# Turning the fetched rows of a routed FFN: TensorE transposes replaced by a trip through memory and a block transpose

## The chip, the cores and the metric

The kernel runs on one core of a Trainium2 chip. The metric is the device time of one execution in microseconds (us); the time of a kernel is the median of its runs. A core has five engines that run beside each other, each through its own list of instructions in order: TensorE (PE in the profile; its weight loads are listed as PEld), VectorE (DVE), ScalarE (ACT), GpSimd (POOL) and SyncE (SP), which issues most of the transfers. Transfers run on 16 DMA engines; SP, ACT and POOL each have a queue of their own into them.

## The reference

The first part is attention with pooled queries: 8 batches, 8 heads, 1152 keys, head size 64, all in f32. Neighbouring queries are averaged in pairs, so 576 queries are left.

```python
q_pool = q.reshape(B, H, S // 2, 2, D).mean(axis=3)
attn = softmax(scale * q_pool @ k.T)          # per batch and head
x = (attn @ v), heads side by side            # (8, 576, 512)
```

The second part is a routed feed-forward network (FFN). In each batch the 128 of the 576 rows with the highest score are updated, and the others are kept as they are.

```python
scores = x @ w_gate
top_idx = np.argpartition(-scores[b], 128)[:128]
xe = x[b, top_idx]                            # 128 rows of 512
h = np.maximum(xe @ w1, 0.0)                  # w1: 512 x 1024
ye = h @ w2                                   # w2: 1024 x 512
out[b, top_idx] = xe + sigmoid(scores[b, top_idx])[:, None] * ye
```

## The kernel before

**Attention.** The work goes by pairs of heads, 4 pairs a batch and 32 in all, and each pair by two halves of 288 queries; so there are 64 halves, `h` in `run`. In a half PE computes the scores of all keys (`scores`, L883, 72 recorded matmuls of 64x64 tiles) and ACT turns them into exponents (L890). PE then multiplies the exponents of the half before by the values (`weighted`, L901), and ACT copies the result out of PSUM (L909). POOL and DVE sum the exponents (L922, L927, L937); DVE turns results with block transposes of 32x32 (L980, and L770 and L774 for the next pair's keys and queries). PSUM is handed out by `banks()` in turn from four tiles.

**The order of the work** is written out by hand. One half emits, in this order: scores, the groups or sums of an earlier pair on ACT (L952 or L967), a place called "mid", the folding of the exponents, a place called "sums", the next pair's keys and queries, weighted, and a place called "end". Each batch has one generator, `routed`, which does its routing and FFN piece by piece. `units` lets it run at a place until it yields the next mark: "mid" and "sums" name the place at which it goes on, and `True` stands for "end". So where the generator yields decides in which half, and behind which instructions, a piece lies on each engine.

**Routing.** For a batch the generator ranks the rows by counting larger scores on DVE (L1159 to L1178), sends the ranks through memory so that every partition holds all of them (L1208 and L1212, on SP), and searches the row of each rank (L1243). It then fetches the 128 chosen rows from the output in memory with an indirect transfer on POOL, the gather (L1270), into `xe`, one row a partition. The rows were put there by `stored` (L1038, SP). In the last batch the ranks go through PE instead (L1220, L1229).

**Before the FFN the rows must be turned**, since a matmul sums over partitions: `xeT` holds the 512 features in four chunks `c` of 128 partitions, and the 128 rows beside each other. Four transposes on PE (L1288) do it, and ACT copies them from PSUM (L1291). In batches 0 to 5 this stands at "mid", two halves after the gather. Feature `c * 128 + p` lies on partition `p` of chunk `c`, and the weights w1 are loaded to match (L691).

**FFN.** Batches 0 to 5 are taken two at a time: `layers_of_two` makes sums of quarters on POOL (L1400), seven products in place of eight on PE (L1434), copies on ACT (L1442), and sums on DVE (L1447). Batches 6 and 7 run alone through `layers` (L1309, L1329). Updated rows go back by an indirect transfer on POOL (L1376).

**The tail.** After the last half `run` lists the rest by hand: `older` is the unit of batches 4 and 5, `old` that of batch 6, `new` that of batch 7, and `pieces(unit, n)` lets a unit run for n yields. There DVE copies batch 7's scores (L1140), counts its ranks (from L1168) and compares (L1220); PE turns these into indices (L1229), and batch 7's gather follows. Batch 6's transposes lie on PE between batch 5's second layer (L1434) and batch 6's first (L1309).

Of the kernel before, what the change touches and what calls it, by code (L numbers as in the profile page):

```python
# [10 lines left out]
P = 128  # L11
BLK = 32

G = 3
F32 = mybir.dt.float32
# [12 lines left out]
def _any_scores(  # L28
# [451 lines left out]
    in_pair = [(j, t) for j in range(2) for t in range(NF)] + [(0, NF)]  # L480
    upcoming = load_pair(*pairs[0])
    run(prepare_pair(upcoming))
    preparing = iter(())
    routing = iter(())
# [23 lines left out]
    for n, (b, hp) in enumerate(pairs):  # L508
        pair = upcoming
        run(preparing)  # L510
        if hp == 0:
            x = xpool.tile([P, NT, Dm], F32, name="x")
        for i, (j, t) in enumerate(in_pair):
            now = {"pair": pair, "j": j, "t": t, "x": x}
            advance(now)
            if two is not None and two["t"] == NF and two["pair"]["hp"] == NPAIR - 1:
                run(routing)
                routing = routed(two["pair"]["b"], two["x"])
            one, two = now, one
            if i == 0 and n + 1 < len(pairs):  # L520
                upcoming = load_pair(*pairs[n + 1])
                preparing = prepare_pair(upcoming)
            if n == 0 and i == 0:
                load_weights()
            if i >= 3:
                next(preparing, None)
            next(routing, None)
    for _ in range(2):
        advance(None)
        one, two = None, one  # L530
    run(routing)
    run(routed(B - 1, x))


class _Plain:
# [152 lines left out]

    def weight_loads(self):

        w1 = self.w1_in.rearrange("(c p) f -> p c f", p=P)  # L691
        w2 = self.w2_in.rearrange("(c p) d -> p c d", p=P)
        for c in range(0, self.NFC, 2):
            yield self.nc.sync.dma_start(self.w2[:, c : c + 2, :], w2[:, c : c + 2, :])
        for c in range(self.ND):
            yield self.nc.sync.dma_start(self.w1[:, c, :], w1[:, c, :])
# [375 lines left out]
    def routed(self, b, part):  # L1072


        nc, ffn, Sp, NT, NF = self.nc, self.ffn, self.Sp, self.NT, self.NF
        tiles = [(t, P if t < NF else self.TAIL) for t in range(NT)]
        mid = "mid" if b < self.B - 2 else True
# [136 lines left out]
        for s0, w in self.slots:  # L1214
            index = ffn.tile([P, 1], I32, name="index", bufs=4)
            own_gate = ffn.tile([P, 1], F32, name="own_gate", bufs=4)
            if b == self.B - 1:

                pick = ffn.tile([P, NT, P], F32, name="pick", bufs=1)
                nc.vector.tensor_tensor(  # L1220
                    out=pick[:, :, 0:w],
                    in0=self.token_line[:, s0 : s0 + w, 0].unsqueeze(1).broadcast_to([P, NT, w]),
                    in1=rank[:, :].unsqueeze(2).broadcast_to([P, NT, w]),
                    op=ALU.is_equal,
                )
                yield True
                ps = self.banks()[:, 0, 0:2]
                for t, rows in tiles:
                    nc.tensor.matmul(  # L1229
                        ps[0:w, :],  # L1230
                        lhsT=pick[0:rows, t, 0:w],
                        rhs=meta[0:rows, t, :],
                        start=(t == 0),
                        stop=(t == NT - 1),
                    )
                nc.scalar.copy(index[0:w, :], ps[0:w, 0:1])
                nc.scalar.copy(own_gate[0:w, :], ps[0:w, 1:2])
            else:
                yield True

                def search(of, to):
                    at = ffn.tile([P, NT, P], F32, name="pick", bufs=1)
                    nc.vector.scalar_tensor_tensor(  # L1243
                        out=at.rearrange("p t i -> p (t i)").rearrange("p (i t) -> p i t", t=NT)[0:w],
                        in0=lines[0:w, :, 0, :],
                        scalar=self.token[0:w, s0 // P : s0 // P + 1],
                        in1=of[0:w, :, :],
                        op0=ALU.is_equal,
                        op1=ALU.mult,
                        accum_out=to[0:w, :],  # L1250
                    )

                found = self.small.tile([P, 1], F32, name="found_token")
                search(self.token_line, found)
                nc.vector.tensor_scalar(
                    out=index[0:w, :],
                    in0=found[0:w, :],
                    scalar1=float(b * Sp),
                    scalar2=None,
                    op0=ALU.add,  # L1260
                )
                if b == self.B - 2:
                    search(lines[:, :, 1, :], own_gate)

                yield "sums" if b < self.B - 2 else True
            if b == self.B - 1:
                xe = ffn.tile([P, self.Dm], F32, name="lines", bufs=1)
            else:
                xe = ffn.tile([P, self.Dm], F32, name="xe", bufs=3)
            nc.gpsimd.indirect_dma_start(  # L1270
                out=xe[0:w, :],
                out_offset=None,
                in_=rows_out,
                in_offset=bass.IndirectOffsetOnAxis(ap=index[0:w, 0:1], axis=0),
                bounds_check=(b + 1) * Sp - 1,
                oob_is_err=False,
            )
            yield True
            if b < self.B - 2:
                search(lines[:, :, 1, :], own_gate)  # L1280
                yield True
            if b != self.B - 2:
                yield mid

            xeT = ffn.tile([P, self.ND, P], F32, name="xeT")
            pv = self.banks()[:, 0, :].rearrange("p (c n) -> p c n", n=P)
            for c in range(self.ND):
                nc.tensor.transpose(  # L1288
                    pv[:, c, 0:w], xe[0:w, c * P : (c + 1) * P], self.ident[0:w, 0:w]
                )  # L1290
            nc.scalar.copy(xeT[:, :, 0:w], pv[:, 0 : self.ND, 0:w])  # L1291
            token = {"xe": xe, "xeT": xeT, "gate": own_gate, "index": index, "rows": rows_out, "w": w, "b": b}
            if b >= self.paired:
                yield mid
                yield from self.layers(token)
            elif b % 2 == 0:
                self.first_of_two = token
            else:
                yield from self.layers_of_two([self.first_of_two, token])
# [259 lines left out]
    def run(self):  # L1559
        nc = self.nc  # L1560
# [11 lines left out]
        sums = self.weight_sums() if self.paired else iter(())  # L1572
        for h in range(n_halves):
            n, s = divmod(h, 2)
# [22 lines left out]
            if h > 1:  # L1597

                of = halves[h - 2 - s]["pair"]
# [33 lines left out]
        def pieces(unit, n=None):  # L1633
            for i, _ in enumerate(unit):
                if i + 1 == n:
                    break
# [3 lines left out]
        old = left.pop() if left else iter(())  # L1640
        older = left.pop() if left else iter(())
        assert not left
        self.gated(halves[-3])
        self.weighted(halves[-1])
        self.drained(halves[-1])
        self.multiplied(halves[-2])
# [7 lines left out]
        _, new, _ = self.routing.pop()  # L1654

        pieces(new, 1)
        for half in (halves[-3], halves[-1]):
            self.divided(half["pair"])
            self.stored(half["pair"])
        pieces(older, 2)  # L1660
        pieces(new, 1)
        pieces(older, 1)
        pieces(new, 3)
        pieces(old, 1)
        pieces(older, 4)
        pieces(old, self.NFC // 2)
        pieces(new, 1)
# [73 lines left out]
```

## Time and profile before

| | us |
|---|---|
| median of three runs | 689.79 (689.55 to 689.9) |
| the profiled execution | 694.23 |
| its span, from first to last instruction | 692.4 |
| PE busy in the span | 683.8 (99%), 10000 matmuls |
| DVE busy | 530.3 (77%) |
| ACT busy | 461.5 (67%) |
| POOL busy | 514.8 (74%) |
| L1288, the transposes before the FFN, batches 0 to 6 | 4.6 busy, 28 matmuls |
| L1291, their copies, all batches | 4.6 busy, 8 copies of 0.573 |
| mean clock granted to PE | 0.996 of full speed |

The page gives busy time by engine and by line. A chain of work that ended last is followed back from the last instruction, at each step to what released it. Lists in order of time give, for one stretch, the start, the duration, engine, line and operation, the tile written and the tile read, their shapes (partitions x elements), how many instructions were merged, and in brackets how long the engine had been idle before and what ended that. An engine with idle time isn't a bound; a bound engine's chain has none.

### The profile page before, as it was taken

The numbers are of one execution on the slowest core, as the hardware profiler recorded it, in microseconds if no ns is written. First come the engines' busy times: TensorE is split into PE (matmuls) and PEld (weight loads), VectorE is DVE, ScalarE is ACT, GpSimd is POOL, SyncE is SP. The second block draws the span as 40 slices with busy tenths as digits, with TensorE's granted clock in tenths as the row PEclk, the third lists the DMA queues.
The fourth block names the chain that finished last, engine by engine and source line by source line (L and its number), as shares of the span: only waits on it lengthen the run. The fifth ranks groups of instructions, "written<-read, shape, count | busy, mean of one in ns | idle before, by whom it ended". The sixth has DMA issues, their size and how long they took to land.

```text
span 692.4 us, 23690 instructions
## 1 busy us (share of the span) xinstructions
PE 683.8 (99%) x10000; PEld 531.5 (77%) x10000; DVE 530.3 (77%) x837; ACT 461.5 (67%) x1005; POOL 514.8 (74%) x503
## 2 busy tenths in 40 slices
PE   8999999999999999999999999999999999999996
PEld 5667899989777978786768877777667885877876
DVE  3867888997999696686598986595868997589830
ACT  4677778777877773857777777583877777576220
POOL 4778888887897793866998888383989888559241
PEclk9999999999999999999999999999999999999999
DMA  8888888687868887743968787763597878344211
GB/s 166 154 172 168 175 185 181 145 152 151 162 137 164 165 151 132 205 90 71 214 122 182 123 174 128 132 175 69 119 199 174 141 154 157 80 115 118 51 47 36
DMA packets 392197, 97.56 MB, mean 141 GB/s; under 512 B 376977, under 2 KB 377105, under 8 KB 390801
## 3 DMA queue, kind: packets, MB, share of 16 engines
q1 hardware_dynamic: 390624, 91.46, 65.4%
q0 software_dynamic: 1296, 4.20, 1.9%
q8 instruction: 80, 1.31, 0.8%
q10 hardware_dynamic: 160, 0.30, 0.2%
q14 instruction: 37, 0.29, 0.2%
HBM read 80.13 MB, written 15.78 MB: 139 GB/s over the span
## 4 chain that ended last, share of the span: by engine, by line
PE 95%; DMA 2%; issue 1%; POOL 1%; ACT 0%; POOLq 0%; SPq 0%; DVE 0%
PE ps L901 41%; PE ps L883 41%; PE ps L1434 11%; PE ps L1309 1%; DMA out_dram<-xe,index 1%; DMA p<-in_k_dram 1%; PE ps L1288 1%; DMA out_dram<-lines,index_part 0%; POOL out_dram L1376 0%; PE ps L850 0%; PE ps L833 0%; ACT p L890 0%; PE ps L1229 0%; POOL xe L1494 0%; PE ps L1131 0%
## 5 line engine op out<-in xcount | busy, mean ns | idle before, releaser
L890 ACT ACTIVATE p<-ps 128x576 f32<-128x576 f32 x576 | 320.4, 693 | 4.9 <-PE ps L883 4.9
L922 POOL TENSOR_TENSOR acc<-p 128x576 f32<-128x576 f32 x192 | 274.2, 1456 | 31.8 <-ACT p L890 31.3
L883 PE MATMUL ps<-qT,kT 64*64 64x288 f32 x4608 | 296.9, 405 | 0.7 <-DVE token L637 0.5
L901 PE MATMUL ps<-p,v_sb 64*64 64x288 f32 x4608 | 295.4, 403 | 0.0
L883 PEld LDWEIGHTS ps<-qT,kT 64*64 64x64 f32 x4608 | 211.9, 133 | 70.0 <-ACT p L890 10.4
L901 PEld LDWEIGHTS ps<-p,v_sb 64*64 64x64 f32 x4608 | 215.2, 133 | 65.1 <-ACT p L890 11.4
L927 DVE TRANSPOSE_TENSOR_REDUCE fold<-p 128x54 f32<-128x1728 f32 x64 | 126.0, 1969 | 41.6 <-ACT p L890 40.9
L927 DVE TRANSPOSE_TENSOR_REDUCE fold<-acc 128x54 f32<-128x1728 f32 x64 | 124.7, 1949 | 22.9 <-POOL acc L922 22.8
L909 ACT COPY two<-ps 128x576 f32<-128x576 f32 x64 | 40.8, 638 | 135.7 <-PE ps L901 121.7
L911 POOL TENSOR_TENSOR av<-two 128x288 f32<-128x288 f32 x64 | 51.2, 800 | 81.1 <-ACT two L909 78.5
L990 POOL TENSOR_TENSOR prod<-avb,w_gate 128x288 f32<-128x288 f32 x64 | 51.3, 802 | 0.2
L980 DVE STREAM_TRANSPOSE avb<-av 128x288 f32<-128x288 f32 x64 | 29.0, 454 | 26.8 <-POOL av L911 23.9
L767 POOL TENSOR_TENSOR qp<-qb 128x576 f32<-128x576 f32 x31 | 43.7, 1409 | 7.8 <-DMA qb<-in_q_dram 7.8
L770 DVE STREAM_TRANSPOSE kT<-kb 128x1152 f32<-128x1152 f32 x31 | 42.0, 1356 | 0.0
L967 ACT ACTIVATE sums<-total,tiny 32x18 f32<-32x18 f32 x124 | 38.2, 308 | 4.6 <-DVE total L958 2.8
L1027 POOL TENSOR_TENSOR x<-avb,rec 128x576 f32<-128x576 f32 x30 | 34.8, 1159 | 0.0
L1178 DVE SCALAR_TENSOR_TENSOR pick<-sc_row,gate_sc,before 128x128 f32<-128x128 f32 (+1 forms) x40 | 32.0, 800 | 1.4
L952 ACT COPY groups<-sum 32x36 f32<-32x36 f32 x124 | 27.0, 218 | 2.9 <-DVE sum L937 1.3
L1049 DVE TENSOR_REDUCE red<-prod 128x9 f32<-128x288 f32 x64 | 27.7, 433 | 0.1
L1442 ACT COPY s<-ps 128x256 f32<-128x256 f32 (+1 forms) x27 | 11.4, 447 | 20.8 <-PE ps L1434 20.8
L937 DVE TENSOR_REDUCE sum<-fold 128x18 f32<-128x108 f32 x64 | 21.9, 342 | 2.2
L1442 ACT COPY hT<-ps 128x512 f32<-128x512 f32 (+1 forms) x15 | 7.9, 545 | 23.2 <-PE ps L1434 21.3
(136 smaller groups left out, 498.9 us busy)
## 6 DMA issues: line engine op xcount, KB each, us to landing
kb<-in_k_dram SPq DMA_DIRECT2D x124, 144.0 KB
qb<-in_q_dram SPq DMA_DIRECT2D x124, 144.0 KB
v_sb<-in_v_dram SPq DMA_DIRECT2D x124, 144.0 KB
tw<-tw SPq DMA_DIRECT2D x10, 1024.0 KB
out_dram<-x SPq DMA_DIRECT2D x128, 72.0 KB
lines<-row_rank SPq DMA_DIRECT2D x7, 640.0 KB
w<-in_moe_w_dram SPq DMA_DIRECT2D x8, 512.0 KB
tw<-tw SPq DMA_DIRECT2D x8, 512.0 KB
```

Source lines behind the costliest of these rows:

```text
L767: nc.gpsimd.tensor_tensor(out=qp[:, :, :], in0=pair["q"][:, :, 0, :], in1=pair["q"][:, :, 1, :], op=ALU.add)
L770: nc.vector.transpose(kT.rearrange("p (c g i) -> p c g i", c=self.NC, i=BLK), pair["k"].rearrange("p (g c) d -> p c g d", c=self.NC),)
L883: nc.tensor.matmul(sc[keys, j, 0:n], lhsT=pair["kT"][rows, c * P + keys.start : c * P + keys.stop], rhs=pair["qT"][rows, qs], start=True, ...
L890: nc.scalar.activation(p[:, c // G, c % G, :, :], sc[:, :, 0:n], AF.Exp, scale=self.scale)
L901: nc.tensor.matmul(av[j * self.D : (j + 1) * self.D, e, 0:n], lhsT=half["pair"]["v"][keys, j, c, :], rhs=half["p"][keys, c // G, c % G, j, :],
L909: nc.scalar.copy(two[:, :, :], av[:, :, 0:n])
L911: nc.gpsimd.tensor_tensor(out=half["av"][:, :], in0=two[:, 0, :], in1=two[:, 1, :], op=ALU.add)
L922: nc.gpsimd.tensor_tensor(out=acc[:, u, :], in0=units[:, 0, u, :], in1=units[:, 1, u, :], op=ALU.add)
L927: nc.vector.tensor_reduce(fold[:, a, :], of.rearrange("p u (m d) -> p (u m) d", d=BLK), AX.X, ALU.add, apply_transpose=True,)
L967: self.nc.scalar.activation(tot[rows, :], pair["total"][:, j * self.QB : (j + 1) * self.QB], AF.Identity, bias=self.tiny[0:BLK, 0:1],)
L990: self.nc.gpsimd.tensor_tensor(out=pair["prod"][:, ns, :], in0=pair["avb"][:, ns, :], in1=self.w_gate[:, hp : hp + 1, :].broadcast_to([P, ...
L1434: nc.tensor.matmul(args[0], lhsT=args[1], rhs=args[2], start=k == 0, stop=k == n - 1)
```

## The change

The rows of batches 0 to 6 are no longer turned on PE. After the gather, a first transfer writes `xe` to a buffer in memory, cut into four blocks of 128 features (512 pieces of 512 bytes). A second one reads it back so that partition `a * 32 + j` holds rows 4j to 4j+3 of block `a` (128 pieces of 2 KB). One block transpose on DVE then writes `xeT` from it. For batches 0 to 5 the transfers are issued by ACT, at "mid" of the half after the gather and at "mid" of the next half, and the transpose stands at "sums" of that same half. For batch 6 SP issues them, and the three steps are placed in the tail by three calls of `pieces(old, 1)`.

A feature now lies on another partition: feature `4p + c` on partition `p` of chunk `c`. So w1 is loaded by `(p c)` instead of `(c p)`, and the last batch, which keeps its four transposes on PE, reads every fourth feature of `xe` for each of them.

In the first six batches the buffer on the way back is the tile `pick`, which the ranks and searches use; in batch 6 it is a tile `kb` of the keys.

```diff
-        w1 = self.w1_in.rearrange("(c p) f -> p c f", p=P)
+        w1 = self.w1_in.rearrange("(p c) f -> p c f", p=P)
...
             yield True
-            if b < self.B - 2:
+            early, n = b < self.B - 2, P // BLK
+            if early:
                 search(lines[:, :, 1, :], own_gate)
-                yield True
-            if b != self.B - 2:
+                yield "mid"
+            if b != self.B - 1:
+                queue = nc.scalar if early else nc.sync
+                copy = self.dram.tile([n, P, P], F32, name="copy")
+                queue.dma_start(
+                    copy[:, 0:w, :].rearrange("a s m -> s a m"), xe[0:w, :].rearrange("s (a m) -> s a m", a=n)
+                )
+            xeT = ffn.tile([P, self.ND, P], F32, name="xeT")
+            if b != self.B - 1:
+                yield "mid" if early else True
+                if early:
+                    moved = ffn.tile([P, NT, P], F32, name="pick", bufs=1)
+                else:
+                    moved = self.load.tile([P, self.KB, BLK], F32, name="kb")
+                moved = moved.rearrange("p t n -> p (t n)")[:, 0 : self.Dm]
+                queue.dma_start(moved, copy.rearrange("a (j b) m -> (a j) (b m)", b=n))
+                yield "sums" if b < self.B - 2 else True
+                nc.vector.transpose(
+                    xeT.rearrange("p c (j b) -> p c b j", b=n),
+                    moved.rearrange("p (b i c) -> p c b i", b=n, c=self.ND),
+                )
+            else:
                 yield mid
-
-            xeT = ffn.tile([P, self.ND, P], F32, name="xeT")
-            pv = self.banks()[:, 0, :].rearrange("p (c n) -> p c n", n=P)
-            for c in range(self.ND):
-                nc.tensor.transpose(
-                    pv[:, c, 0:w], xe[0:w, c * P : (c + 1) * P], self.ident[0:w, 0:w]
-                )
-            nc.scalar.copy(xeT[:, :, 0:w], pv[:, 0 : self.ND, 0:w])
+                pv = self.banks()[:, 0, :].rearrange("p (c n) -> p c n", n=P)
+                of = xe.rearrange("p (n c) -> p c n", c=self.ND)
+                for c in range(self.ND):
+                    nc.tensor.transpose(pv[:, c, 0:w], of[0:w, c], self.ident[0:w, 0:w])
+                nc.scalar.copy(xeT[:, :, 0:w], pv[:, 0 : self.ND, 0:w])
...
         self.gated(halves[-3])
+        pieces(old, 1)
         self.weighted(halves[-1])
...
         pieces(new, 1)
+        pieces(old, 1)
         for half in (halves[-3], halves[-1]):
             self.divided(half["pair"])
             self.stored(half["pair"])
         pieces(older, 2)
         pieces(new, 1)
+        pieces(old, 1)
         pieces(older, 1)
         pieces(new, 3)
-        pieces(old, 1)
         pieces(older, 4)
```

## The prediction, made before the result was known

> **What bounds the kernel now.** I read the profiled execution first: it took 694.23 us, its span is 692.4 us, so 1.83 us lie around the span. The three plain runs have a median of 689.79 us, 4.44 us less. Every sum below is made in the profile's time and then taken off the median; I take the difference of 4.44 us to be the same for both kernels. A difference of 0.2% (1.4 us) is about what a measurement of this kernel can tell from no change.
>
> Next the page: its chain of work that ended last, then the same chain inside one stretch that holds the transposes of batch 2.
>
> ```profile
> PE 95%; DMA 2%; issue 1%; POOL 1%; ACT 0%; POOLq 0%; SPq 0%; DVE 0%
> ```
>
> ```profile
> 341.32 4.37 PE ps L883 x72
> 345.69 0.59 PE ps L1288 x4
> 346.27 4.53 PE ps L901 x72
> 350.80 4.37 PE ps L883 x72
> 355.17 4.37 PE ps L901 x72
> 359.53 4.36 PE ps L883 x72
> ```
>
> The columns are start, duration, line and number of instructions. TensorE (PE) carries 95% of the chain, and inside a half-pair it is never idle: scores (L883), then weighted values (L901), then the next scores. A half without other work lasts 359.53 - 350.80 = 8.73 us. The half with the four transposes of L1288 lasts 350.80 - 341.32 = 9.48 us. So the four transposes cost PE 0.75 us: 0.59 us of their own, and the L901 behind them takes 4.53 instead of 4.37. PE's own timeline gives the same for batches 0, 1, 3 and 5 (9.56, 9.56, 9.48 and 9.59 us from one L883 to the next). Batch 4's half is 10.05 us for other reasons, below. The granted clock is 0.996 throughout, so the clock takes no part.
>
> **The change, part by part.**
>
> *Removed from PE and ScalarE (ACT).* Batches 0 to 6 lose four transposes and the bank they took; ACT loses the copy L1291 (0.57 us). In batches 0, 1, 2, 3 and 5 PE is the bound on both sides of the transposes, so each gives 0.75 us: 5 x 0.75 = -3.75 us. What is late next in these halves is ACT: the weight loads before L901 already wait 0.17 to 0.3 us for its exponents, so I count no slack behind L909, the copy with which ACT begins each half's work on PE's results.
>
> *Batch 4.* Here ACT is late already:
>
> ```profile
> 504.95 0.92 ACT L952 COPY groups<-sum 32x36 f32<-32x36 f32 x4
> 508.35 0.64 ACT L909 COPY two<-ps 128x576 f32<-128x576 f32 x1 [2.48 <-issue]
> ...
> 516.03 1.27 ACT L967 ACTIVATE sums<-total,tiny 32x18 f32<-32x18 f32 x4 [1.70 <-DVE total L958]
> 517.32 0.85 ACT L952 COPY groups<-line 32x18 f32<-32x18 f32 x4
> 518.08 0.57 ACT L1291 COPY xeT<-ps 128x512 f32<-128x512 f32 x1
> 518.56 0.62 ACT L909 COPY two<-ps 128x576 f32<-128x576 f32 x1
> ```
>
> The numbers in brackets are idle time and who ended it. ACT waits 1.70 us for VectorE (DVE), and L909 then follows L1291 with no gap. If PE comes 0.75 us earlier, L909 doesn't: the time becomes PE's wait. I count 0 for batch 4.
>
> *Added to ACT: two transfers for each of batches 0 to 5.* The first is issued in the middle of the half after the gather, behind the groups L952, and waits there for the gathered rows. Behind it on ACT stands L909, and PE waits for L909 through the exponents. The gather (L1270) lands 3.5 to 6.2 us after its start. Batch by batch, landing against the next L909: 171.5 against 174.2; 243.3 (median 4.4 assumed) against 245.4; 338.6 against 341.4; 407.5 against 412.4; 500.89 + 6.2 = 507.1 against 508.35; 574.5 against 580.0. All land in ACT's idle time. The issue itself costs between two rows:
>
> ```profile
> 0.79 0.99 ACTq L794 DMA_DIRECT2D p<-in_q_dram  x2
> 508.29 7.30 SPq L742 DMA_DIRECT2D kb<-in_k_dram  x4
> ```
>
> That is 0.5 us each in the only two that ACT issues today, 1.8 us each in SyncE's (SP's) slowest group. I take 0.7 us, nearest to the 0.65 us of a store of 576 pieces (L1038, 2.61 us for four), since the copy has 512 pieces of 512 bytes. At 0.7 us ACT is free in time everywhere, with 0.5 us left in batch 4. At 1.8 us batch 4 loses 0.6 us. The second transfer comes one half later, where L1291 was, 9 us after the first, and waits for nothing that late; it is 0.1 us longer than the copy it replaces, and only batch 4 has no idle time behind it. Sum for ACT's issues: +0.4 us taken, 0 to +2 us.
>
> *Added to DVE: the block transpose.* 512 elements a partition, both sides in steps of four elements. The contiguous transposes (288 elements 454 ns, 576 in 728) give 0.67 us. The one row with a strided side, L1140, copies 288 elements in 696 ns where the contiguous copies (192 in 358, 384 in 552) give 455: 0.84 ns per element more. With that on one side it is 1.1 us, on both 1.5; I take 1.1.
>
> The Trainium skill ("SBUF — State Buffer", Door 1) says that each access which crosses to a new 16-byte line pays a penalty. A step of four f32 does so every time; L1140's row agrees in direction. By the rule the low end of 0.67 us would go.
>
> In the main loop this transpose stands behind the half's fold (L937), about 5 us after the second transfer's issue, so it waits for nothing. DVE's next readers lie one half off. In odd batches GpSimd's L1400 reads xeT: in batch 1 it starts at 256.65 us and would wait for 258.1 + 1.1 = 259.2; PE needs the first of its sums only after its own first product, at 261.0. In batches 3 and 5 L937 ends 1.2 us before L1400. Cost 0 on PE.
>
> The Trainium skill's rule against the change: "VectorE: DVE Perf Modes", section "Rules for kernel authors", has a 128x128 transpose done on TensorE where PSUM will do. By it the transposes stay where they are and the sum is 0; by the rows here they lie on the bound engine while DVE is 77% busy.
>
> *The tail, batch 6.* Here SP issues both transfers and DVE's transpose stands between the score copy L1140 and the rank counts of the last batch.
>
> ```profile
> 627.81 0.35 SPq L1208 DMA_DIRECT2D row_rank<-both  x1
> 629.60 0.32 SPq L1212 DMA_DIRECT2D lines<-row_rank  x1
> 634.29 1.90 DVE L1243 SCALAR_TENSOR_TENSOR pick<-lines,token,token_line 128x640 f32<-128x640 f32 x1 [1.35 <-DMA lines<-row_rank]
> 641.09 1.13 POOL L1270 DMA_INDIRECT xe<-out_dram,index  x1
> 651.17 0.81 DVE L1168 TENSOR_SCALAR_CACHE_REDUCE pick<-sc_row,gate_sc 128x576 f32<-128x576 f32 x1 [1.64 <-ACT gate_sc L682]
> 658.08 1.33 DVE L1220 TENSOR_TENSOR pick<-token_line,rank 128x640 f32<-128x640 f32 x1
> 659.96 1.26 PE L1229 MATMUL ps<-meta,pick 128*128 128x2 f32 x10
> ```
>
> The gather lands 3.6 us after its start, at 644.7. The rank line's round trip prices the legs: 1.79 us out for 5 KB, 4.7 us back for 640 KB. At the 245 GB/s of the fullest stretch I measured (335 to 345 us), 256 KB take 1.07 us: 2.9 us out, and back 4.7 less 1.6 for the bytes that aren't there, 3.1. The rows are back at 650.7, and the transpose ends at 651.8. L1168 began at 651.17, so the rank counts, L1220 and its reader L1229 move by 0.6 us, to about 660.1 where PE now has them at 659.96, while PE itself could be there 0.75 us sooner. Net +0.15 us. Landing before 650.0 hides the transpose (-0.45); at 653 the tail loses 2.4 us. SP's eight stores behind the second issue go at about 648.6 instead of 648; their reader, the last gather at 661.69, has over 4 us to spare.
>
> *The last batch's four transposes* stay on PE but read every fourth element. No row shows a strided weight load. L1288's loads take 0.14 us each; between nothing and twice that, 0 to +0.55 us on PE. I take +0.2, since the loads partly lie beside the matmuls. Loading w1 in another row order moves the same 4 KB rows: 0.
>
> **Sum:** -3.75 + 0 + 0.4 + 0.15 + 0.2 = -3.0 us. 689.79 - 3.0 = **686.8 us**. Its own range runs from every doubtful term at its best (six batches, -4.5, tail -0.45: 684.8) to +1.6 more on ACT or in the tail (688.4).
>
> **Rivals.**
>
> *1. ACT becomes the bound (slower than before).* The place is the issue between L952 and L909. Its price is whatever passes the idle time there: 1.4 to 2.5 us at the first issue, 0.9 to 2.0 plus the 0.57 of L1291 at the second, nothing in batch 4. If each issue holds ACT for about 3 us (or the gathers land 2 us later), each batch loses 0.5 to 1 us at each issue, some 6 us with batch 4, and the gain of 3.75 is gone: about 692.0. It decides from about 2.6 us an issue. For it: SP's 1.8 us when the queues are full. Against: 0.5 us in ACT's own rows.
>
> *2. The tail pays back the loop.* The trip of batch 6 takes longer than 6 us, as the longest wait of L1109 on its small row (4.1 us) allows; DVE stands still with the last batch's ranks behind it. At 652 to 654 us instead of 650.7 the tail's term is +1.4 to +3.4 instead of +0.15, and the sum -1.8 to +0.3: about 689.0.
>
> *3. The transposes weren't worth 0.75 us*, since ACT's exponents set the half: gain under 0.2%, 689.5. Against it: halves without transposes do run in 8.73.
>
> **How the numbers follow.** Forecast (686.8, a gain of over 1.4 us) 0.70; rival 1 0.15, slower; rival 2 0.10 and rival 3 0.05, both within 0.2%. So faster 0.70, same 0.15, slower 0.15. The range takes in the forecast's own, rivals 2 and 3 and the near end of rival 1: 684.7 to 690.2.
>
> **What would show it.** Right: halves after a gather at 8.7 to 8.8 us with no L1288; ACT issues under 1 us that end before L909; DVE's transpose near 1.1 us without a wait in the loop; L1229 of the tail waiting for DVE. Wrong: idle PE before L883 or L901 put down to ACT just behind the new transfers, or the tail's transpose waiting past 652 us.

## The result, and the profile after

The changed kernel takes 695.28 us (median of 8 runs, 693.01 to 697.55), the kernel before 689.89 us (8 runs beside them, 689.55 to 691.05). The ratio is 1.0075, with a 95% interval of 1.0059 to 1.0091: slower by some 5 us, where 3 us less were forecast. A later run of the same two kernels (kernel 11 below) gave 1.0081 (1.0062 to 1.0101).

The profiled execution took 697.45 us with a span of 695.7 us, against a span of 692.4 before. Line numbers move a little: the copy out is L1286, the read-back L1297, the block transpose L1299, the last batch's transposes L1308; the sums on GpSimd (POOL) are L1418 and the seven products L1452. SP's lines keep their numbers.

The chain that ended last, from the page after, by engine:

```profile
PE 81%; DMA 7%; POOL 4%; SPq 3%; issue 2%; DVE 1%; ACT 1%; POOLq 0%; ACTq 0%
```

TensorE (PE) held 95% of this chain before; now transfers hold 7% and SyncE's queue (SPq) 3%. ACT, which was to be the danger, holds 1%.

The removed transposes are really gone from PE's path. The chain of the changed kernel in the stretch of batch 2 (start, duration, line and number of instructions):

```profile
343.23 4.37 PE ps L883 x72
347.60 4.38 PE ps L901 x72
351.98 4.37 PE ps L883 x72
```

This half lasts 351.98 - 343.23 = 8.75 us, where it lasted 9.48. So time came in elsewhere. To find the place, I compare the start of the weighted values (L901) of each of the 64 halves with the kernel before, both counted from half 8. At the halves of the six batches the difference falls by 0.78, 0.67, 0.73, 0.73, 1.04 and 0.73 us, 4.68 us in all. But at the loop's end it stands at +4.91 us, so 9.6 us net were lost in between. The four largest rises are +2.94 us from half 19 to 23, +2.17 us from half 26 to 27, +4.1 us in halves 38 and 39 and +1.7 us around half 55, 10.9 us together; some other halves give 1.3 us back. The rest of the span adds up: the profiled execution before had reached its first weighted values 1.42 us later (20.18 against 18.76), ahead of anything the change touches, and the tail is 0.2 us shorter: -1.4 + 4.9 - 0.2 = +3.3 us.

What is late at those places is SP's loads. The list of what SP's queue waited for, after (total us, times, longest):

```profile
SPq L742 <- DMA pick<-copy: 16.1, 3, 6.5
SPq L756 <- DMA copy<-xe: 15.0, 4, 4.5
...
SPq L1038 <- DMA copy<-xe: 11.0, 2, 5.5
...
SPq L1038 <- DMA pick<-copy: 3.8, 1, 3.8
```

With 2.8 us at L745 these are 48.7 us, some 8 us a batch, and none of them was there before. L742 and L756 load keys and values, L1038 stores results: none of them has anything to do with the data of `copy<-xe` or `pick<-copy`, which ACT issues. Here is SP in batch 0, after (start, time issuing, line, number of transfers):

```profile
165.58 6.55 SPq L756 DMA_DIRECT2D v_sb<-in_v_dram  x4
172.23 2.64 SPq L1038 DMA_DIRECT2D out_dram<-x  x4
181.48 3.13 SPq L742 DMA_DIRECT2D kb<-in_k_dram  x3
```

and ACT in the same stretch:

```profile
167.88 0.41 ACTq L1286 DMA_DIRECT2D copy<-xe  x1
...
178.83 0.36 ACTq L1297 DMA_DIRECT2D pick<-copy  x1
```

The same stretch of SP before:

```profile
171.30 3.12 SPq L756 DMA_DIRECT2D v_sb<-in_v_dram  x4
174.52 2.65 SPq L1038 DMA_DIRECT2D out_dram<-x  x4
177.27 3.81 SPq L742 DMA_DIRECT2D kb<-in_k_dram  x4
```

The four value loads took 3.12 us before and take 6.55 now, and the next keys no longer follow the stores at once. SP issues the first one at 165.58, then stands until 170.85, which is when ACT's copy, issued at 167.88, has landed. Behind the stores SP stands again until 181.48, 2.6 us after ACT issued the read-back.

The single instructions of the trace name what is waited for. A semaphore is a counter on which an engine can wait. Each transfer has one or more that its engine waits on before it issues, and one that the transfer counts up when it lands:

| start us | engine, transfer | waits on | counts up |
|---|---|---|---|
| 165.58 | SP, first value load | 102 and 103 | 103 |
| 167.88 | ACT, `copy<-xe` | 111 (the gather's) | **105** |
| 170.85 | SP, second value load | **105** | 105 |
| 171.24 | SP, third value load | 106 | 106 |
| 171.71 | SP, fourth value load | 107 | 107 |

So the second value load waits for the semaphore that the copy counts up. In the whole trace SP's and ACT's transfers count up the same eight semaphores (100, 101, 103 to 107, 109: 72 to 75 transfers of SP on each), in turn in the order of the program; GpSimd's transfers have others (111 to 118). As the table shows, a transfer is issued only when the one that had its semaphore before, eight places earlier, has landed. Among SP's own transfers in the kernel before, no load or store of the loop shows up as waiting for another one's landing in this way. ACT's copy takes a place in this turn among loads which SP issues some 8 us before ACT comes to it, and then the copy waits for the gather: SP has run on, meets the copy's semaphore eight transfers later, and stands still with everything behind it.

PE notices where the values or the queries come too late. PE in batch 3, after (in brackets the idle time and who ended it):

```profile
382.91 0.70 PE L901 MATMUL ps<-p,v_sb 64*64 64x288 f32 x4 [0.36 <-DMA v_sb<-in_v_dram]
384.74 6.03 PE L901 MATMUL ps<-p,v_sb 64*64 64x288 f32 x66 [1.13 <-DMA v_sb<-in_v_dram]
```

Such waits of PE for values come to 5.1 us, and there were none before; POOL's wait for queries (L767) went from 7.8 to 16.5 us. SP has little to catch up with: before the change, one pair's set of sixteen transfers kept it busy for 16 us (161.28 to 177.27) and the next set for 13.9 us (177.27 to 191.13), of a pair's 17.5.

### The profile page after: what moved, and what is told of

Its sections match the earlier page's. It is cut to its first block, busy times and chain, and to the rows that moved or that the text cites. A ratio compares the mean times of both kernels' runs of the same rounds, so it can differ in the third digit from the quotient of the medians.

```text
span 695.7 us, 23662 instructions
## 1 busy us (share of the span) xinstructions
PE 682.6 (98%) x9972; PEld 567.0 (81%) x9972; DVE 535.8 (77%) x844; ACT 457.7 (66%) x998; POOL 516.3 (74%) x503
## 2 busy tenths in 40 slices
DMA packets 396900, 101.23 MB, mean 146 GB/s; under 512 B 377200, under 2 KB 380912, under 8 KB 395504
## 3 DMA queue, kind: packets, MB, share of 16 engines
q0 software_dynamic: 1296, 4.20, 1.8%
q10 hardware_dynamic: 4192, 3.44, 1.7%
## 4 chain that ended last, share of the span: by engine, by line
PE 81%; DMA 7%; POOL 4%; SPq 3%; issue 2%; DVE 1%; ACT 1%; POOLq 0%; ACTq 0%
PE ps L901 35%; PE ps L883 33%; PE ps L1452 11%; POOL acc L922 2%; DMA v_sb<-in_v_dram 2%; DMA out_dram<-xe,index 1%; DMA qb<-in_q_dram 1%; SPq L745 1%; PE ps L1327 1%; DMA copy<-xe 1%; SPq L756 1%; DVE fold L927 1%; DMA lines<-row_rank 1%; ACT p L890 1%; PE ps L616 1%
## 5 line engine op out<-in xcount | busy, mean ns | idle before, releaser
L901 PE MATMUL ps<-p,v_sb 64*64 64x288 f32 x4608 | 300.4, 405 | 5.4 <-DMA v_sb<-in_v_dram 5.1
L901 PEld LDWEIGHTS ps<-p,v_sb 64*64 64x64 f32 x4608 | 234.9, 133 | 56.4 <-ACT p L890 14.9
L883 PEld LDWEIGHTS ps<-qT,kT 64*64 64x64 f32 x4608 | 230.8, 132 | 50.7 <-ACT p L890 5.2
L909 ACT COPY two<-ps 128x576 f32<-128x576 f32 x64 | 40.8, 638 | 145.6 <-PE ps L901 138.1
L767 POOL TENSOR_TENSOR qp<-qb 128x576 f32<-128x576 f32 x31 | 43.7, 1410 | 16.5 <-DMA qb<-in_q_dram 16.5
L774 DVE STREAM_TRANSPOSE qT<-qp 128x576 f32<-128x576 f32 x31 | 22.7, 731 | 4.5 <-POOL qp L767 4.5
L1460 ACT COPY s<-ps 128x256 f32<-128x256 f32 (+1 forms) x27 | 11.4, 447 | 20.9 <-PE ps L1452 20.9
```

The source lines that it names most:

```text
L767: nc.gpsimd.tensor_tensor(out=qp[:, :, :], in0=pair["q"][:, :, 0, :], in1=pair["q"][:, :, 1, :], op=ALU.add)
L883: nc.tensor.matmul(sc[keys, j, 0:n], lhsT=pair["kT"][rows, c * P + keys.start : c * P + keys.stop], rhs=pair["qT"][rows, qs], start=True, ...
L901: nc.tensor.matmul(av[j * self.D : (j + 1) * self.D, e, 0:n], lhsT=half["pair"]["v"][keys, j, c, :], rhs=half["p"][keys, c // G, c % G, j, :],
L909: nc.scalar.copy(two[:, :, :], av[:, :, 0:n])
```

## The experiments

The theory: the trip is cheap, and the loss is SP's waits on semaphores which it shares with ACT's transfers. The rivals: the bytes of the trip (101.23 MB after, 97.56 before) compete with the loads; DVE's transpose delays its queue; the tail loses. The first four kernels ran on one chip, the next four on a second, the last three on a third; each ratio is to the kernel before on the same chip. A ratio and the quotient of two medians can differ by some 0.2%.

**1. No trip in the loop.** Both transfers of batches 0 to 5 are left out, and DVE turns the rows where they lie, so the rows of `xeT` are not the right ones.

```diff
-                queue.dma_start(copy[:, 0:w, :]..., xe...)
+                if not early:
+                    nc.sync.dma_start(copy[:, 0:w, :]..., xe...)
...
-                queue.dma_start(moved, copy...)
+                if not early:
+                    nc.sync.dma_start(moved, copy...)
...
-                    moved.rearrange("p (b i c) -> p c b i", b=n, c=self.ND),
+                    (xe if early else moved).rearrange("p (b i c) -> p c b i", b=n, c=self.ND),
```

> This kernel leaves out both transfers of batches 0 to 5; VectorE's block transpose reads the fetched rows where they lie, so the rows of xeT are not the right ones, while every other instruction keeps its place. Theory A (SyncE's loads stand still behind the ACT transfers, since the program has them count on the same eight completion semaphores in turn): without the transfers nothing holds SyncE, and only the gain is left, six times 0.75 us: about 685.5 us, 0.65% under the kernel before. Rival B (the extra traffic): the same, since the traffic is gone too. Rival C (VectorE's transpose is what delays the halves): it is still there, so 693 to 695 us.

Measured: 687.53 us, ratio 0.9959 (0.9945 to 0.9973). SP waits for no transfer of ACT. Everything else of the change, with DVE's transposes and the tail, is worth about 2.8 us by the ratio and 4.1 us by the medians (691.58 us before on this chip): about what I had forecast for the whole, and less than the 0.65% expected of this kernel. The loss comes with the transfers.

**2. The same transfers of one piece.** As above, but ACT issues transfers of 512 bytes at the same places.

```diff
+                if early:
+                    queue.dma_start(copy[0, 0:1, :], xe[0:1, 0:P])
...
+                if early:
+                    queue.dma_start(moved[0:1, 0:P], copy[0, 0:1, :])
```

> As the kernel without the trip, but ACT issues a transfer of one piece of 512 bytes out and back at the places of the two removed ones; VectorE again transposes the rows where they lie, so part of the data is not the right one. Theory A: the waits are the same though nothing worth naming is moved, so nearly all of the loss comes back: 692 to 695 us, and SyncE waits some 40 us in total for the two. Rival B (traffic): 3.7 MB less are moved, so it stays at 685 to 687 us.

Measured: 692.81 us, ratio 1.0018 (0.9995 to 1.004), 0.59% more than without them, with 98.09 MB moved, practically the same as without (98.08). SP's waits are back, 29.9 us in all where some 40 were expected:

```profile
SPq L742 <- DMA pick<-copy: 16.0, 3, 5.6
SPq L1038 <- DMA copy<-xe: 8.6, 2, 4.6
SPq L1038 <- DMA pick<-copy: 3.8, 1, 3.8
```

Six kilobytes cost 4 us by the ratios, 5 by the medians. Bytes can't be the reason for that part.

**3. GpSimd issues the transfers**, the copy at "sums" in place of "mid".

```diff
-                yield "mid"
+                yield "sums"
...
-                queue = nc.scalar if early else nc.sync
+                queue = nc.gpsimd if early else nc.sync
```

> The whole change, with the transfers of batches 0 to 5 issued by GpSimd (the first one at the place called sums instead of mid); its transfers count on other semaphores than those of SyncE. Theory A: SyncE waits for none of them, all the bytes are moved, and the time falls under the kernel before, to 686 to 688 us, unless GpSimd's own issues cost more than its idle time. Rival B (traffic): no better than the changed kernel, 693 to 696 us.

Measured: 689.28 us, ratio 0.9983 (0.9956 to 1.001), all 101.23 MB moved. That is clear of the changed kernel's 1.0075, but it can't be told from no change and misses the 686 to 688 us expected. SP waits for no copy or read-back in the loop. In its profile one half of batch 1 loses 2.17 us by itself. DVE and PE there:

```profile
260.19 1.11 DVE L1299 STREAM_TRANSPOSE xeT<-pick 128x512 f32<-128x512 f32 x1
```

```profile
258.88 2.05 PE L1452 MATMUL ps<-xeT,w 128*128 128x128 f32 x16
262.16 4.06 PE L1452 MATMUL ps<-s,tw 128*128 128x128 f32 x34 [1.23 <-POOL s L1418]
```

POOL's sums wait for the transpose, and PE for the sums. The prediction had seen this wait and priced it at 0 on PE; it had the transpose begin at 258.1 us, and with DVE 2 us later than that (260.19) the wait reaches PE.

**4. SP issues the transfers itself**, the copy at "mid" as before and the read-back at the end of the same half. In SP's own list both stand behind a pair's loads and stores.

```diff
-                queue = nc.scalar if early else nc.sync
+                queue = nc.sync
...
-                yield "mid" if early else True
+                yield True
```

> The whole change, with all transfers issued by SyncE itself, both behind the stores of a pair. SyncE then waits in its own order, for the first transfer's 2.7 us only, in place of 8 to 10 us for each batch in the changed kernel. Theory A: most of the loss is gone, 687 to 690 us. Rival B (traffic): 693 to 696 us. Rival D (ACT's time for the issues): ACT is free of them as well, 686 us.

Measured: 692.3 us, ratio 1.0011 (0.9982 to 1.0041), which can't be told from no change. It lies above the range of theory A and below that of rival B. SP waits for no copy at its loads, but 15.5 us at the read-backs for the copies (7 times, the tail's among them). That such a trip doesn't suit a queue with 14 to 16 us of work in 17.5 is the likely reason that no gain is left; no run shows it.

**5. Only the transfers.** The kernel before with its transposes on PE, and ACT's 512-byte transfers added.

```diff
-                yield True
+                yield "mid"
+                copy = self.dram.tile([4, P, P], F32, name="copy")
+                nc.scalar.dma_start(copy[0, 0:1, :], xe[0:1, 0:P])
...
+                nc.scalar.dma_start(moved[0:1, 0, :], copy[0, 0:1, :])
```

> The kernel before with its transposes kept on TensorE; ACT only adds, for batches 0 to 5, two transfers of 512 bytes at the changed kernel's places, whose data nobody reads. Theory (SP's loads wait for completion semaphores that they share with ACT's transfers): SP's loads wait some 5 us a batch for these tiny transfers, and the kernel is slower than before by the difference of the one-piece kernel and the kernel without a trip: about +4 us, ratio 1.005 (1.003 to 1.008). Rival (the bytes of the trip, or the block transpose on DVE, make the loss): 1.000 to 1.001, since ACT's issues took 0.38 and 0.33 us.

Measured: 693.78 us, ratio 1.0037 (1.0025 to 1.0049). Twelve transfers that nobody reads make the kernel before slower by 2.6 us. SP's list shows the same waits, 33.0 us in all:

```profile
SPq L742 <- DMA pick<-copy: 13.6, 3, 5.6
...
SPq L1038 <- DMA copy<-xe: 7.5, 2, 4.0
...
SPq L756 <- DMA copy<-xe: 6.5, 3, 2.5
```

**6. GpSimd's queue, batch 1 on PE.**

```diff
+            trip = b not in (1, self.B - 1)
...
-                yield "mid"
-            if b != self.B - 1:
-                queue = nc.scalar if early else nc.sync
+                yield "sums" if trip else True
+            if trip:
+                queue = nc.gpsimd if early else nc.sync
...
-            if b != self.B - 1:
+            if trip:
```

> GpSimd's queue for the transfers as before, but batch 1 is turned by TensorE (every fourth element, two halves after the gather). Theory (with GpSimd's queue what is lost is batch 1's sums on GpSimd, which waited 2 us for DVE's transpose): the 2.2 us of batch 1's half go and 0.3 us of strided transposes come, so about 1.9 us less than the GpSimd kernel: ratio 0.9956 (0.993 to 0.9975). Rival (the bytes and GpSimd's issues cost something in each batch): ratio 0.998, no better than with all six batches.

Measured: 689.18 us, ratio 0.9967 (0.9955 to 0.9979). Faster than before; half 27 loses nothing. That it gains over kernel 3 is not shown, since the intervals overlap.

**7. Three batches only** (`trip = b in (0, 2, 4, self.B - 2)`, otherwise as 6).

> GpSimd's queue, but only for batches 0, 2 and 4; 1, 3 and 5 are turned by TensorE with every fourth element. Theory: three batches at -0.75 us, three at +0.25 us (four weight loads of 0.20 in place of 0.14 us), the tail even: -1.5 us, ratio 0.998 (0.996 to 0.9995). If batches 3 and 5 lose to DVE's transpose as batch 1 did, it is as good as the kernel with all batches but 1, or better.

Measured: 690.22 us, ratio 0.9988 (0.9979 to 0.9997), 0.8 us where 1.5 were expected: the sign is sure, and the ratio is inside the expected range.

**8. The tail alone** (`trip = b == self.B - 2`).

> Only batch 6 goes through memory; batches 0 to 5 are turned by TensorE with every fourth element, two halves after the gather. No transfers of ACT. Theory: SP waits for no transfer of ACT in the loop; the tail is even; six batches pay +0.25 us each for strided weight loads: ratio 1.002 (1.000 to 1.003). Rival (the tail's trip or w1's other order makes a good part of the loss of 5 us): 1.004 or more.

Measured: 691.56 us, ratio 1.0007 (0.9998 to 1.0016): so neither the tail nor the other row order of w1 makes the loss. Strided weight loads cost less than I expected. The loads of the batches (ns: least, median, most):

```profile
L1309 PEld LDWEIGHTS ps<-ident,xe x24: 195/209/218, 178.6 to 583.8; 128*128 128x128 f32 x24
```

They took 141 ns before, and four of them are 0.27 us longer. But in five of the six batches the half with them is later by only 0.04 to 0.1 us (in batch 4 it is earlier): most of it lies beside matmuls.

**9. One word.** The changed kernel with the same places, and GpSimd as the issuer.

```diff
-                queue = nc.scalar if early else nc.sync
+                queue = nc.gpsimd if early else nc.sync
```

> The changed kernel with one word altered: the transfers of batches 0 to 5 are issued by GpSimd, at the same two places as ACT issued them. Theory (the semaphores shared by SP and ACT): SP waits for no copy or read-back in the loop, and the kernel is faster than the changed one by at least half of its loss: ratio to before 0.998 (0.995 to 1.003), the upper end if GpSimd's sums stand behind a copy that waits for the gather. Rival (place or bytes of the trip make the loss): as slow as the changed kernel, 1.006 to 1.009.

Measured: 689.75 us, ratio 0.9968 (0.9955 to 0.9981). The changed kernel on the same chip (11) has 1.0081, so one word is worth 1.1%, about 7.8 us. SP's loads wait for engines again, as before the change:

```profile
SPq L756 <- PE ps L901: 23.9, 5, 14.0
...
SPq L745 <- POOL qp L767: 15.0, 6, 5.0
SPq L756 <- PE ps L883: 14.5, 18, 1.9
```

**10. ACT, at the place of kernel 3.**

```diff
-                yield "mid"
+                yield "sums"
```

> The changed kernel with the copy at the place that the first GpSimd kernel used, sums instead of mid, still issued by ACT. Theory: the order of the transfers in the program and so their semaphores stay the same, ACT only comes to the copy later; SP waits at least as long as in the changed kernel, ratio 1.008 (1.005 to 1.014). Rival (the first GpSimd kernel gained by its place): 0.998 to 1.002.

Measured: 699.64 us, ratio 1.011 (1.0095 to 1.0124). The place was not what helped kernel 3. The expectation of longer waits was wrong: SP's waits for the copies are 44.4 us, not more than 48.7. Beside kernel 11 on the same chip they are as long (44.8 us). Whether this kernel is really slower than the changed one, by 2 us in the medians, is not shown, since the intervals overlap (1.0095 to 1.0124 against 1.0062 to 1.0101); why it might be is open.

**11. The changed kernel again**, on the same chip as 9 and 10.

> The changed kernel itself, on the same chip as the two kernels beside it: 1.0075 (1.006 to 1.009) as in the first comparison.

Measured: 697.62 us, ratio 1.0081 (1.0062 to 1.0101), SP's waits 44.8 us.

Side by side, how far the profiled executions' halves are behind the kernel before (us, all counted from half 8), and SP's waits for copies and read-backs in the loop:

| half | after | 1 no trip | 2 one piece | 5 only transfers | 9 GpSimd |
|---|---|---|---|---|---|
| 19 | -1.39 | -0.60 | 0.68 | 0.43 | -0.93 |
| 23 | 1.55 | -1.05 | 4.08 | 2.68 | -1.41 |
| 37 | 2.51 | -2.61 | 2.82 | 3.41 | -2.24 |
| 39 | 6.57 | -2.60 | 5.13 | 3.41 | -2.11 |
| 49 | 5.63 | -3.33 | 4.19 | 3.56 | -1.71 |
| 63 | 4.91 | -5.74 | 2.86 | 3.02 | -2.00 |
| SP's waits | 48.7 | 0 | 29.9 | 33.0 | 0 |

Only the kernels with ACT's transfers end behind the kernel before. All three lose 2.3 to 3.4 us between halves 19 and 23; in halves 38 and 39 the changed kernel and kernel 2 lose again, and kernel 5 doesn't. These are single executions, which differ by a us or two where nothing was changed (halves 14 to 15), so sizes are taken from the ratios. The size of the loss isn't the sum of SP's waits but what of them is left when PE gets to the values.

What stays open is how the loss divides. Tiny transfers cost 0.37% in kernel 5 and 0.59% between kernels 1 and 2; the queue as a whole is worth 1.1% between 9 and 11. The rest of 0.5 to 0.8% shows only where full-sized transfers meet the shared semaphores: in kernel 9 the same bytes leave the gain almost whole (0.9968 against 0.9959 without a trip, on different chips). That a larger copy lands later and holds SP longer (48.7 us of waits against 29.9) fits this, but no run separates it. One rival can be looked up: ACT's queue carried the trip in 4032 packets (4192 against 160 without it), GpSimd's in 960 (2256 against 1296), so the trip's packets might slow the loads. But once issued, SP's loads landed as fast beside them: medians of 4.5 us for keys, 3.7 for queries and 3.5 for values in the changed kernel, 4.4, 3.6 and 3.6 in kernel 9.

## Why the prediction was wrong

**The step that failed** is the one that began "Added to ACT: two transfers ... waits there for the gathered rows. Behind it on ACT stands L909". It looked for what is queued behind the waiting transfer on ACT's own list and found idle time there. That was true, and not enough: the transfers also stand in one line with SP's for eight semaphores, and behind them there stood SP's value and key loads, on a queue with little slack. The sum has no term for this wait, so it stood at 0. ACT's transfers in place of GpSimd's cost 7.8 us, by the one word of kernel 9 against 11. Kernel 5 shows 2.6 us of it for the wait with nothing but tiny transfers added; how much of the rest is the same wait stays open.

The prediction's own signs would not have found it. Of its signs of being right, halves of 8.75 us without L1288, issues under 1 us that end before L909 and DVE's transposes near 1.1 us without a wait in the loop all came true. Its sign of being wrong, PE waiting for ACT, hardly showed: PE waited 5.1 us for SP's values, and no sign named SP's loads.

The trace of before could have raised the question, though not answered it. In its loop ACT issued no transfer, so no row of it shows an SP load behind one of ACT's. But its single instructions show that SP's transfers wait on the semaphores which they count up themselves, and that ACT's two loads at the start count up two of the same eight (100 and 106).

**Rival 1** had the right sign and the wrong mechanism. ACT's issues took 0.38 us (copy) and 0.33 us (read-back), under the 0.7 us assumed. In batch 0 the L909 behind the copy started at 172.23 us, after 2.48 us in which ACT was idle and waited for PE; the L909 behind the read-back after 1.03 us of the same. PE's list of waits names ACT's exponents for 0.2 us in L901. Its weight loads waited 14.9 us for them, against 11.4 before and 12.1 in kernel 1; but where most was lost, at the late values of half 38, ACT itself stood 5.76 us waiting for PE ahead of L909.

**The transposes on PE** were worth 0.75 us a batch as forecast: five halves fell by 0.67 to 0.78 us. Batch 4, counted as 0 because ACT was late there, fell by 1.04 us; in all 4.68 us came instead of 3.75. Kernels 1 and 11 show the same fall there (1.05 and 1.04 us), while kernel 5, which keeps the transposes, falls by 0.30 us in that half. So about 0.75 us are the transposes here too, and the 0 for batch 4 was wrong; the other 0.3 us are the one execution of the kernel before. Rival 3 is out.

**DVE's block transpose** took 1.18 us (1.13 in the tail) against 1.1 assumed, so the value from L1140's strided row held. That DVE's transpose hides in the loop held in the changed kernel, whose PE waits for none of the sums. It does not hold where DVE is late (batch 1 of kernel 3: 1.23 us of wait on PE).

**The tail** was called +0.15 us and was 0.2 us shorter in the profile; kernel 8 bounds it together with the strided loads at 1.0007 (0.9998 to 1.0016). DVE in the tail, after:

```profile
653.44 1.13 DVE L1299 STREAM_TRANSPOSE xeT<-kb 128x512 f32<-128x512 f32 x1 [0.59 <-DMA kb<-copy]
...
654.75 0.81 DVE L1168 TENSOR_SCALAR_CACHE_REDUCE pick<-sc_row,gate_sc 128x576 f32<-128x576 f32 x1
```

Less the 3.49 us by which the loop ended later, the transpose begins at 649.95 and L1168 at 651.26, where it stood at 651.17 before. So the trip fits, and rival 2 is out. What the last batch's strided loads cost, +0.2 us assumed, no run shows by itself; in kernel 8's loop four of them cost 0.04 to 0.1 us.

**The sum without the failed step** would have held: 686.8 of 689.79 us is 0.9957, and the change without its transfers measured 0.9959, with them on GpSimd's queue 0.9968. That it comes so close is partly luck: batch 4's transposes were counted at 0 and gave 0.75 us, the tail was 0.35 us better than its term, and ACT's issues, counted at 0.4 us, are not in kernel 1 at all.

## What to carry to other kernels

Before a transfer is put on another engine's queue, ask which counters it shares with the queue that feeds the bound engine, not only what stands behind it on its own engine: a transfer that has to wait for data can hold up loads that have nothing to do with it. Look for it after the change in the list of what the loading queue waited for: a load that waits for a transfer of other data is the sign. If the transfer must wait, issue it from a queue that shares no counters with the loads, here GpSimd's, and read the cost of that (0.84 and 0.59 us an issue) in that engine's slack.

## What the runs showed of the hardware

The Trainium skill ("DMA: Bandwidth & Descriptors", section "Issuing engines are not separate DMA queues") says that starting transfers from several engines saves only the sequencer's time, since all of them run on the same 16 DMA engines. Here the choice of the engine mattered far more than its issue time: the same bytes at the same two places took 1.0081 of before by ACT and 0.9968 by GpSimd, though GpSimd's issues were the dearer ones (0.84 and 0.59 us against 0.38 and 0.33) and its copies landed later (4.8 us after their issue against 2.6, medians). That doesn't contradict the page: what the runs show at work is this program's sharing of semaphores between SP and ACT (2.6 us in kernel 5), and SP's loads landed as fast in both kernels.

A weight load of 128x128 f32 that reads every fourth element took 0.20 to 0.22 us (median 0.21), a contiguous one 0.14. A block transpose on DVE of 512 f32 elements a partition, in steps of four elements on both sides, took 1.11 to 1.24 us.
